# k' one slot sooner, token-MLP stages re-slotted, relu of k on ScalarE, tables by iota and ScalarE

## The chip, the cores and the metric

One core of a Trainium2 chip. The metric is device time in microseconds (us) of one execution; the median of a few executions is the kernel's time. A profiled execution gives the span (first to last instruction) and the times of the single instructions.

## What is computed

Two parts, for 8 batches of 576 tokens, 8 heads of 64. First linear attention with position weights:

```python
r = np.maximum(x, 0.0)                       # x is q or k
phi = np.concatenate([r * c, r * s], -1)     # c, s = cos, sin of (pi/2) * pos / S
kv  = einsum('bhsf,bhsd->bhfd', k_p, v);  z = k_p.sum(2)
x   = einsum('bhsf,bhfd->bhsd', q_p, kv) / (einsum('bhsf,bhf->bhs', q_p, z) + 1e-6)
```

Then, with x as batch x 576 x 512, a mixing over tokens and an output product:

```python
W_tok = scale * einsum('bsd,btd->bst', x @ w_q, x @ w_k)
out   = np.maximum(einsum('bst,btd->bsd', W_tok, x), 0.0) @ w_out
```

All inputs and the output are float32; the kernel computes in bf16 with float32 sums.

## The kernel before, in words

**Units of work.** A *slot* g is one pair of heads of one batch: 32 slots, four to a batch (Bc = g // 4 is the batch, r = g % 4 the place in it). Loads and the elementwise preparation go by halves H = g // 2, that is two slots at a time (16 halves).

**Preparation of a half** (lines 173 to 211). `relu_k` makes rk = relu(k) in bf16, `mul_k` multiplies rk by the table `cossin` on VectorE and gives k' (tile kp, bf16, 128x2304), `cast_v` gives v in bf16 in one of three v buffers, and `dup_q` writes relu(q) twice side by side (tile qd). In the loop before, relu_k, cast_v and dup_q of half H+2 all run on GpSimd (POOL), issued in slot 2H, and mul_k of half H+1 runs on VectorE (DVE) in slot 2H+1, after that slot's other VectorE work. rk, kp and qd have two buffers each, the raw inputs four.

**A slot** (lines 215 to 258). `qk_pe(g)` issues 18 small matmuls k'^T v (needs kp and v) and 18 transposes of qd into the one buffer qk_ps. VectorE then copies k'v out (kv_sb) and multiplies the transposed q by the table cst (qpt). `num(g-1)` issues 12 matmuls of the slot before, and VectorE takes the reciprocal (rec) and the product x_sb.

**The token MLP of a batch** (lines 260 to 355) goes in stages, each a group of matmuls into the PSUM tag m2, which has two buffers in turn, and one copy out of it on ScalarE (ACT): xT (transposes of x, one stage for each half of a batch), wk (x w_k, tile wkj), wq (tile wqT), kx (wkj^T x), mx (four stages: two row halves i by two column halves nh; the relu goes with the copy, tile mix_sb), and wout (row tiles of 128 output rows, four matmuls each, copied to o_sb and stored by two DMAs per row tile from SyncE, SP). A pair of batches has 9 row tiles, 4 in the even batch's share and 5 in the odd one's.

**The order** is the program's own: the loop of lines 378 to 420 sets which stage is issued in which slot, and every engine and the SP queue work strictly in that order. Before, in the slots of batch Bc: r=0 and r=1 have the four mx stages of batch Bc-2, one ahead and one behind qk_pe; xT (second half of the batch before) is in r=1, wk and wq in r=2, kx in r=3 with xT of this batch's first half; wout pieces of batch Bc-3 stand in r=0, 1 and 2. After the loop (lines 422 to 438) a tail finishes the rest: mx of batch 6, the wout pieces of batches 5, 6 and 7, and all MLP stages of batch 7. SP's queue holds in this order the loads (load(H+3) in each even slot) and the stores of the wout pieces.

**The start** (lines 84 to 155): loads, 16 warm-up matmuls, and the tables: POOL counts by iota, VectorE makes them into angles and spreads cosine and sine over the table, ScalarE takes the sine.

Of the kernel before, what the change touches and what calls it, by code (L numbers as in the profile page):

```python
# [24 lines left out]
def kernel(  # L25
# [10 lines left out]
    nc = tc.nc  # L36
# [58 lines left out]
    warm_up(16)  # L95

    wq_f = consts.tile([P, NDM, DH], FP32)
    wk_f = consts.tile([P, NDM, DH], FP32)
    wo_f = consts.tile([P, NDM, DM], FP32)

    ident = consts.tile([P, P], BF16)
    make_identity(nc, ident)

    r_i = consts.tile([P, C9], I32)
    nc.gpsimd.iota(r_i, pattern=[[1, C9]], base=0, channel_multiplier=C9)
    t_i = consts.tile([P, C9, D], I32)
    nc.gpsimd.iota(t_i, pattern=[[1, C9], [C9, D]], base=0, channel_multiplier=0)
    r_f = consts.tile([P, C9], FP32)
    nc.vector.tensor_copy(r_f, r_i)
    g5_f = consts.tile([P, C9], FP32)  # L110
    nc.vector.tensor_scalar(g5_f, r_f, float(S) - 0.5, float(S),
                            op0=ALU.is_ge, op1=ALU.mult)
    s_f = consts.tile([P, C9], FP32)
    nc.vector.tensor_sub(s_f, r_f, g5_f)
    coef = math.pi / 2.0 / S
    u_f = consts.tile([P, C9], FP32)
    nc.vector.tensor_scalar(u_f, s_f, -coef, math.pi / 2.0, op0=ALU.mult, op1=ALU.add)
    cos_t = consts.tile([P, C9, 1], FP32)
    sin_t = consts.tile([P, C9, 1], FP32)
    nc.scalar.activation(cos_t, u_f, AF.Sin, bias=0.0, scale=1.0)  # L120
    nc.scalar.activation(sin_t, s_f, AF.Sin, bias=0.0, scale=coef)
    cossin = consts.tile([P, C9, 2, D], BF16)
    nc.vector.tensor_copy(cossin[:, :, 0, :], cos_t.to_broadcast([P, C9, D]))
    nc.vector.tensor_copy(cossin[:, :, 1, :], sin_t.to_broadcast([P, C9, D]))

    t_f = consts.tile([P, C9, D], FP32)
    nc.vector.tensor_copy(t_f, t_i)
    nc.vector.tensor_scalar(t_f[0:64], t_f[0:64], -1.0, float(S),
                            op0=ALU.mult, op1=ALU.add)
    cst = consts.tile([P, C9, D], BF16)  # L130
    nc.scalar.activation(cst, t_f, AF.Sin, bias=0.0, scale=coef)
# [40 lines left out]

    def relu_k(H, lo, hi, eng):
        if lo == 0:
            rks[H] = prep.tile([P, 2, C9, D], BF16, name="rk")
        o = rks[H][:, lo:hi].rearrange("p r c d -> p r (c d)")
        if eng is nc.scalar:
            nc.scalar.activation(o, raw["k", H][:, lo:hi, :], AF.Relu)  # L178
        else:
            eng.tensor_scalar(o, raw["k", H][:, lo:hi, :], FMAX, 0.0,  # L180
                              op0=ALU.min, op1=ALU.max)
# [10 lines left out]
    def cast_v(H, lo, hi, eng):  # L192
        src = raw["v", H][:, lo:hi, :].rearrange("p r (c d) -> p r c d", c=C9)
        dst = v_bufs[H % 3][:, lo:hi, :, 0:D]
        if eng is nc.scalar:
            nc.scalar.copy(dst, src)
        else:
            eng.tensor_scalar(dst, src, 1.0, 1.0, op0=ALU.mult, op1=ALU.mult)  # L198

    def dup_q(H, lo, hi, eng):  # L200
        if lo == 0:
            qd[H] = prep.tile([P, 2, C9, 2, D], BF16, name="qd")
        n = hi - lo
        dst = qd[H][:, lo:hi].rearrange("p r c w d -> p (r c) w d")
        src = raw["q", H][:, lo:hi, :].rearrange(
            "p r (c d) -> p (r c) d", c=C9).unsqueeze(2).to_broadcast(
                [P, n * C9, 2, D])
        if eng is nc.scalar:
            nc.scalar.activation(dst, src, AF.Relu)
        else:  # L210
            eng.tensor_scalar(dst, src, FMAX, 0.0, op0=ALU.min, op1=ALU.max)  # L211
# [100 lines left out]
        kxs[b] = kx  # L312

    def mx(b, st, eng):
        i, nh = divmod(st, 2)
        hs = S // 2
        if b % 2 == 0 and st == 0:
            mixs[b // 2] = mixpool.tile([P, NDM, 2 * S], BF16, name="mix_sb")
        mix_sb = mixs[b // 2]
        mx_ps = m2_tile(FP32, "mx_ps")  # L320
        for r in range(2):
            dmc = 2 * r + i
            nc.tensor.matmul(  # L323
                mx_ps[:, r, 0:hs],
                kxs[b][64 * r:64 * r + 64, dmc * P:(dmc + 1) * P],
                wqTs[b][64 * r:64 * r + 64, nh, :], start=True, stop=True)
        c0 = (b % 2) * S + nh * hs
        dst = mix_sb.rearrange("p (r i) n -> p r i n", r=2)[:, :, i, c0:c0 + hs]
        if eng is nc.scalar:
            nc.scalar.activation(dst, mx_ps[:, :, 0:hs], AF.Relu, scale=scale_moe)  # L330
        else:
            eng.tensor_scalar(dst, mx_ps[:, :, 0:hs], scale_moe, 0.0,  # L332
                              op0=ALU.mult, op1=ALU.max)

    def wout(bp, rt0, n, engs):
        o_ps = m2_tile(FP32, "o_ps")
        o_sb = outpool.tile([P, 2, DM], FP32, name="o_sb")
        for r in range(n):
            rt = rt0 + r
            for dmc in range(NDM):  # L340
                nc.tensor.matmul(  # L341
                    o_ps[:, r, :], mixs[bp][:, dmc, rt * P:(rt + 1) * P],
                    wo_sb[:, dmc, :], start=(dmc == 0), stop=(dmc == NDM - 1))
        if len(engs) == 1:
            copy(engs[0], o_sb[:, 0:n, :], o_ps[:, 0:n, :])
        else:
            for r in range(n):
                copy(engs[r], o_sb[:, r, :], o_ps[:, r, :])
        for r in range(n):
            for hi in range(2):  # L350
                bloc, j0 = divmod(P * (rt0 + r) + 64 * hi, S)
                dst = dataclasses.replace(
                    out, offset=out.offset + (2 * bp + bloc) * S * DM + (j0 // 64) * DM,
                    ap=[[C9 * DM, 64], [1, DM]])
                nc.sync.dma_start(dst, o_sb[hi * 64:hi * 64 + 64, r, :])
# [84 lines left out]

# [28 lines left out]
```

## Time and profile before

| what | value |
|---|---|
| median of 3 executions | 162.76 us (161.47 to 163.2) |
| profiled execution, its own time | 162.92 us |
| its span | 161.1 us (1.8 us lie around it) |
| busy in the span: PE, DVE, ACT, POOL | 119.4, 100.9, 72.3, 75.0 us |
| mean granted TensorE clock | 0.906 |
| start of qk_pe in slots 4, 6, 8 | 23.82, 32.63, 42.10 us |
| start of qk_pe in slots 12, 16, 20, 24, 28 | 56.60, 70.86, 87.11, 102.78, 118.95 us |
| start of num(31), the first work of the tail | 131.75 us |

A row of the time line reads: start, duration, engine, line and operation, output<-inputs, and in square brackets how long the engine had been idle before it and what ended that. PE is TensorE, SPq is SyncE's queue of DMA issues. "x18" at a row's end means 18 instructions merged.

### The profile page before, as it was taken

Reading aid. Unit: us, or ns where it says so; the run is one execution under the profiler, and the core shown is the slowest. Engines: PE = TensorE matmul, PEld = TensorE weight load, DVE = VectorE, ACT = ScalarE, POOL = GpSimd, SP = SyncE. Lnnn points to the kernel's source line nnn. Section 1 sums busy time; section 2 is a strip of 40 time slices with the busy share of each in tenths; the row PEclk is TensorE's granted clock in tenths of the full one; section 3 lists DMA queues with packets and bytes.
Section 4 is the critical chain, followed back from the end, with each engine's and each line's share of the span. In section 5 each row is a group of like instructions: output and inputs, shape, how many; then the busy total and the mean of one; then the engine's idle time right before and its main releaser. Section 6 shows DMA issues by size and latency. Waiting matters only on the chain.

```text
span 161.1 us, 5016 instructions
## 1 busy us (share of the span) xinstructions
PE 119.4 (74%) x2184; PEld 78.6 (49%) x2184; DVE 100.9 (63%) x163; ACT 72.3 (45%) x96; POOL 75.0 (47%) x68
## 2 busy tenths in 40 slices
PE   6633655599649798979994969797979986996920
PEld 2222654486437555755663537454645663452400
DVE  6668684954794858776757678767576766024210
ACT  3422420211841547475645553764476653634320
POOL 7188269998665556632995366456520000000000
PEclk9995586556995999999999999999999999999996
DMA  5999999999994005499969989995521540278785
GB/s 174 379 379 377 404 412 411 408 410 406 409 402 172 0 4 131 94 285 406 375 140 344 401 322 216 375 410 178 118 51 36 124 109 0 57 164 204 164 194 132
DMA packets 20469, 39.38 MB, mean 244 GB/s; under 512 B 3040, under 2 KB 3040, under 8 KB 20448
## 3 DMA queue, kind: packets, MB, share of 16 engines
q1 hardware_dynamic: 20448, 39.07, 72.6%
q8 instruction: 17, 0.28, 0.7%
q14 instruction: 4, 0.03, 0.1%
HBM read 29.62 MB, written 9.44 MB: 242 GB/s over the span
## 4 chain that ended last, share of the span: by engine, by line
PE 42%; DVE 29%; ACT 7%; DMA 6%; SPq 5%; POOL 3%; issue 3%; ACTq 0%; POOLq 0%
DVE kp L187 14%; PE o_ps L341 14%; DVE x_sb L256 7%; PE qk_ps L223 6%; PE wq_ps L296 6%; DMA kf<-in_k_dram 6%; ACT o_sb L274 5%; PE num_ps L250 5%; PE qk_ps L230 4%; DVE qpt_buf L237 4%; PE wk_ps L282 4%; SPq L81 3%; PE mx_ps L323 2%; POOL qd L211 2%; DVE kv_sb L235 2%
## 5 line engine op out<-in xcount | busy, mean ns | idle before, releaser
L211 POOL TENSOR_SCALAR qd<-qf 128x2304 bf16<-128x2304 f32 (+1 forms) x16 | 33.7, 2109 | 10.2 <-issue 8.6
L223 PE MATMUL qk_ps<-v_buf,kp 64*128 64x65 bf16 x576 | 15.9, 201 | 25.1 <-DVE kp L187 21.3
L341 PE MATMUL o_ps<-wo_sb,mix_sb 128*128 128x512 bf16 x144 | 33.7, 379 | 0.1
L187 DVE TENSOR_TENSOR kp<-rk,cossin 128x2304 bf16<-128x2304 bf16 (+1 forms) x17 | 29.4, 1727 | 2.2 <-ACT rk L178 2.2
L235 DVE CAST kv_sb<-qk_ps 128x130 bf16<-128x130 f32 x32 | 9.4, 293 | 33.1 <-PE qk_ps L230 33.1
L223 PEld LDWEIGHTS <-kp 64*128 64x128 bf16 x576 | 12.3, 100 | 33.2 <-DVE kp L187 26.4
L198 POOL TENSOR_SCALAR v_buf<-vf 128x1152 bf16<-128x1152 f32 (+1 forms) x17 | 20.8, 1222 | 15.8 <-DMA vf<-in_v_dram 15.0
L256 DVE TENSOR_TENSOR x_sb<-num_ps,rec 128x640 bf16<-128x640 f32 x32 | 26.4, 825 | 1.1
L274 ACT COPY o_sb<-o_ps 128x1024 f32<-128x1024 f32 (+1 forms) x20 | 17.6, 885 | 20.7 <-PE o_ps L341 20.7
L180 POOL TENSOR_SCALAR rk<-kf 128x1152 bf16<-128x1152 f32 x15 | 17.7, 1180 | 16.0 <-DVE kp L187 10.3
L237 DVE TENSOR_TENSOR qpt_buf<-qk_ps,cst 128x1152 bf16<-128x1152 bf16 x32 | 23.9, 748 | 0.0
L274 ACT COPY xT_buf<-xT_ps 128x1152 bf16<-128x1152 bf16 x15 | 16.8, 1119 | 13.0 <-PE xT_ps L266 13.0
L330 ACT ACTIVATE mix_sb<-mx_ps 128x576 bf16<-128x576 f32 x28 | 17.7, 654 | 6.7 <-PE mx_ps L323 6.6
L341 PEld LDWEIGHTS <-mix_sb 128*128 128x128 bf16 x144 | 13.4, 98 | 14.1 <-issue 0.5
L250 PE MATMUL num_ps<-kv_sb,qpt_buf 128*128 128x65 bf16 x320 | 17.9, 204 | 0.1
L230 PE MATMUL qk_ps<-ident,qd 64*128 64x64 bf16 x576 | 15.3, 200 | 1.5 <-POOL qd L211 1.5
L250 PEld LDWEIGHTS <-qpt_buf 128*128 128x128 bf16 x320 | 13.7, 103 | 3.2 <-DVE x_sb L256 0.4
L323 PE MATMUL mx_ps<-wqT,kx 64*128 64x288 bf16 x64 | 9.1, 288 | 5.3 <-ACT o_sb L274 2.7
L230 PEld LDWEIGHTS <-qd 64*128 64x128 bf16 x576 | 12.1, 101 | 1.6 <-POOL qd L211 1.6
L266 PE MATMUL xT_ps<-ident,x_sb 128*128 128x128 bf16 x160 | 12.3, 228 | 0.7 <-DVE mix_sb L332 0.7
L266 PEld LDWEIGHTS <-x_sb 128*128 128x128 bf16 x160 | 10.5, 103 | 2.6 <-issue 0.9
L253 PE MATMUL num_ps<-eps_t,ones_t 128*128 128x5 bf16 x64 | 11.2, 176 | 0.0
(52 smaller groups left out, 105.1 us busy)
## 6 DMA issues: line engine op xcount, KB each, us to landing
out_dram<-o_sb SPq DMA_DIRECT2D x72, 128.0 KB, 2.4
kf<-in_k_dram SPq DMA_DIRECT2D x15, 576.0 KB, 9.3
qf<-in_q_dram SPq DMA_DIRECT2D x15, 576.0 KB, 9.6
vf<-in_v_dram SPq DMA_DIRECT2D x15, 576.0 KB, 9.8
wo_f<-in_moe_w_out_dram SPq DMA_DIRECT2D x1, 1024.0 KB, 9.9
kf<-in_k_dram SPq DMA_DIRECT2D x2, 288.0 KB, 3.5
qf<-in_q_dram SPq DMA_DIRECT2D x2, 288.0 KB, 4.0
vf<-in_v_dram SPq DMA_DIRECT2D x2, 288.0 KB, 4.2
```

Source lines behind the costliest of these rows:

```text
L180: eng.tensor_scalar(o, raw["k", H][:, lo:hi, :], FMAX, 0.0, op0=ALU.min, op1=ALU.max)
L187: nc.vector.tensor_mul(kp[H][:, lo:hi], rks[H][:, lo:hi].unsqueeze(3).to_broadcast([P, n, C9, 2, D]), cossin.unsqueeze(1).to_broadcast([P, ...
L198: eng.tensor_scalar(dst, src, 1.0, 1.0, op0=ALU.mult, op1=ALU.mult)
L211: eng.tensor_scalar(dst, src, FMAX, 0.0, op0=ALU.min, op1=ALU.max)
L223: nc.tensor.matmul(kvp[:, hh, :], kp[H][p0:p0 + 64, i, c, :, :], v_bufs[H % 3][p0:p0 + 64, i, c, 0:D + 1], start=(c == 0), stop=(c == C9 - 1))
L230: nc.tensor.transpose(qt[:, hh, c * D:(c + 1) * D], qd[H][p0:p0 + 64, i, c, :, :], ident[p0:p0 + 64, p0:p0 + 64])
L237: nc.vector.tensor_mul(qpt_bufs[g % 3][:, :, 1:SLOTS, :], qt.rearrange("f h (c d) -> f h c d", c=C9), cst.unsqueeze(1).to_broadcast([P, 2, ...
L250: nc.tensor.matmul(nv[:, hh, u, :], qpt_bufs[g % 3][:, hh, 2 * u:2 * u + 2, :], kvs[g][:, hh, :], start=(u == 0), stop=False)
L256: nc.vector.tensor_tensor(xs[b][:, :, 2 * pr:2 * pr + 2, :].rearrange("p u h d -> p h u d"), nv[:, :, :, 0:D], rec.to_broadcast([P, 2, SC, ...
L266: nc.tensor.transpose(xT_ps[:, i, u * P:(u + 1) * P], xs[b][:, u, 2 * hp:2 * hp + 2, :], ident)
L274: nc.scalar.copy(dst, src)
L341: nc.tensor.matmul(o_ps[:, r, :], mixs[bp][:, dmc, rt * P:(rt + 1) * P], wo_sb[:, dmc, :], start=(dmc == 0), stop=(dmc == NDM - 1))
```

## The change

Five edits:

1. `mul_k(H+1)` moves from slot 2H+1 to slot 2H, that is one slot ahead.
2. In the loop relu_k goes to ScalarE; POOL keeps dup_q, now ahead of cast_v. In the first half of the data dup_q goes to POOL and cast_v to VectorE; relu_k of half 1 goes to ScalarE.
3. The MLP stages move: mx of a batch stands in r=3 of the next batch (two stages, column half 0) and in r=0 after it (two, column half 1), behind qk_pe; wk in r=1 behind a wout piece, kx and wq in r=2. The numbering of mx's stages changes so that the first two fill column half 0.
4. The wout pieces of batch Bc-2 (not Bc-3) stand in r=0 (2 row tiles), r=1 (1) and r=3 (1 or 2). The tail therefore loses the five row tiles of batch 5 and two mx stages, and its order changes.
5. The tables are made from iotas by two sine activations on ScalarE with the counts as int32 inputs; eight VectorE instructions fall away. 14 warm-up matmuls, not 16.

```diff
+    for hh in range(2):
+        ph = slice(64 * hh, 64 * hh + 64)
+        nc.gpsimd.iota(ki[ph, :, 0], pattern=[[-1, C9]], base=S, channel_multiplier=-C9)
+        nc.gpsimd.iota(ki[ph, :, 1], pattern=[[1, C9]], base=0, channel_multiplier=C9)
+    nc.gpsimd.iota(qi[0:64], pattern=[[-1, C9], [-C9, D]], base=S, channel_multiplier=0)
+    nc.gpsimd.iota(qi[64:128], pattern=[[1, C9], [C9, D]], base=0, channel_multiplier=0)
...
+    nc.scalar.activation(cossin, ki.unsqueeze(3).to_broadcast([P, C9, 2, D]),
+                         AF.Sin, bias=0.0, scale=coef)
+    nc.scalar.activation(cst, qi, AF.Sin, bias=0.0, scale=coef)
...
     def mx(b, st, eng):
-        i, nh = divmod(st, 2)
+        nh, i = divmod(st // 2 + 2 * (st % 2), 2)
...
     for lo in range(2):
         relu_k(0, lo, lo + 1, A)
-        cast_v(0, lo, lo + 1, G)
-        dup_q(0, lo, lo + 1, A if lo == 0 else G)
+        dup_q(0, lo, lo + 1, G)
+        cast_v(0, lo, lo + 1, V)
         mul_k(0, lo, lo + 1)
     load(2)
-    relu_k(1, 0, 2, G)
+    relu_k(1, 0, 2, A)
+    dup_q(1, 0, 2, G)
     cast_v(1, 0, 2, G)
-    dup_q(1, 0, 2, G)
...
-            return [(bp, 0, 2), (bp, 2, 2)]
-        return [(bp, 4, 2), (bp, 6, 2), (bp, 8, 1)]
+            return [(bp, 0, 2), (bp, 2, 1), (bp, 3, 1)]
+        return [(bp, 4, 2), (bp, 6, 1), (bp, 7, 2)]
...
-        if r == 0 and Bc >= 2:
-            mx(Bc - 2, 0, A)
-        if r == 1 and Bc >= 2:
-            mx(Bc - 2, 2, A)
         qk_pe(g)
-        if r == 0 and Bc >= 2:
-            mx(Bc - 2, 1, A)
-        if r == 1 and Bc >= 2:
-            mx(Bc - 2, 3, A)
+        if r == 3 and Bm >= 0:
+            mx(Bm, 0, A)
+            mx(Bm, 2, A)
+        if r == 0 and Bm >= 1:
+            mx(Bm - 1, 1, A)
+            mx(Bm - 1, 3, A)
         if g >= 1:
             num(g - 1)
-        if g % 2 == 1 and H + 1 < NB:
+        if g % 2 == 0 and H + 1 < NB:
             mul_k(H + 1, 0, 2)
...
-            relu_k(H + 2, 0, 2, G)
+            relu_k(H + 2, 0, 2, A)
+            dup_q(H + 2, 0, 2, G)
             cast_v(H + 2, 0, 2, G)
-            dup_q(H + 2, 0, 2, G)
...
+        if r == 0:
+            wout_piece(Bm - 1, 0)
         if r == 1:
...
+            if Bm >= 0:
+                xT(2 * Bm + 1, A)
+            wout_piece(Bm - 1, 1)
+            if Bm >= 0:
+                wk_stage(Bm, A)
+        if r == 2 and Bm >= 0:
+            kx_stage(Bm, A)
+            wq_stage(Bm, A)
         if r == 3:
...
+            wout_piece(Bm - 1, 2)
             xT(2 * Bc, A)
+    L = B - 1
     num(NG - 1)
+    mx(L - 1, 1, A)
+    mx(L - 1, 3, V)
+    wout_piece(L - 1, 0)
+    xT(2 * L + 1, V)
+    wout_piece(L - 1, 1)
+    wk_stage(L, V)
+    wout_piece(L - 1, 2)
+    wq_stage(L, A)
+    kx_stage(L, V)
+    for st in (0, 2, 1, 3):
+        mx(L, st, A if st < 2 else V)
+    for w in ((L // 2, 4, 2), (L // 2, 6, 2), (L // 2, 8, 1)):
         wout(*w, (A, V))
```

(Bm is Bc - 1; `wout_piece(b, n)` issues the n-th piece of batch b on ScalarE, if b is not negative.)

How it moves the instructions, at three places. First VectorE in slots 4 and 5 (halves: kp here is that of half 3, needed by slot 6). Before:

```order
L235 CAST kv_sb<-qk_ps 128x130
L237 TENSOR_TENSOR qpt_buf_158<-qk_ps,cst 128x2x576
L255 RECIPROCAL rec<-num_ps 128x10
L256 TENSOR_TENSOR x_sb<-num_ps,rec 128x2x5x64
L235 CAST kv_sb<-qk_ps 128x130
L237 TENSOR_TENSOR qpt_buf_160<-qk_ps,cst 128x2x576
L255 RECIPROCAL rec<-num_ps 128x10
L256 TENSOR_TENSOR x_sb<-num_ps,rec 128x2x5x64
L187 TENSOR_TENSOR kp<-rk,cossin 128x2304
L235 CAST kv_sb<-qk_ps 128x130
```

and with the change, for the same two slots:

```order
L221 CAST kv_sb<-qk_ps 128x130
L223 TENSOR_TENSOR qpt_buf_144<-qk_ps,cst 128x2x576
L241 RECIPROCAL rec<-num_ps 128x10
L242 TENSOR_TENSOR x_sb<-num_ps,rec 128x2x5x64
L173 TENSOR_TENSOR kp<-rk,cossin 128x2304
L221 CAST kv_sb<-qk_ps 128x130
L223 TENSOR_TENSOR qpt_buf_146<-qk_ps,cst 128x2x576
L241 RECIPROCAL rec<-num_ps 128x10
L242 TENSOR_TENSOR x_sb<-num_ps,rec 128x2x5x64
L221 CAST kv_sb<-qk_ps 128x130
```

The k' product stood behind all work of slot 5 and directly ahead of the kv_sb copy of slot 6; now it stands at the end of slot 4, with the four instructions of slot 5 between it and slot 6.

Second, ScalarE in the four slots that hold the wout pieces of batch 1 (o_sb): slots 16 to 19 before, from the mx copies of r=0 on:

```order
L330 ACTIVATE mix_sb<-mx_ps 128x2x288 x2
L274 COPY o_sb<-o_ps 128x1024
L330 ACTIVATE mix_sb<-mx_ps 128x2x288 x2
L274 COPY xT_buf_164<-xT_ps 128x2x576
L274 COPY o_sb<-o_ps 128x1024
L274 CAST wkj<-wk_ps 128x640
L274 CAST wqT<-wq_ps 128x576
L274 COPY o_sb<-o_ps 128x512
L274 CAST kx<-kx_ps 128x512
L274 COPY xT_buf_162<-xT_ps 128x2x576
```

and slots 12 to 15 now:

```order
L316 ACTIVATE mix_sb<-mx_ps 128x2x288 x2
L164 ACTIVATE rk<-kf 128x1152
L260 COPY o_sb<-o_ps 128x1024
L260 COPY xT_buf_148<-xT_ps 128x2x576
L260 COPY o_sb<-o_ps 128x512
L260 CAST wkj<-wk_ps 128x640
L164 ACTIVATE rk<-kf 128x1152
L260 CAST kx<-kx_ps 128x512
L260 CAST wqT<-wq_ps 128x576
L316 ACTIVATE mix_sb<-mx_ps 128x2x288 x2
L260 COPY o_sb<-o_ps 128x1024
L260 COPY xT_buf_150<-xT_ps 128x2x576
```

The two relu of k (rk) are new on ScalarE, one in r=0 between the mx copies and the wout copy, one in r=2 ahead of kx; and the output of batch 1 is copied four slots sooner.

Third, ScalarE at the end of the program, from the mx copies of batch 6 on. Before:

```order
L330 ACTIVATE mix_sb<-mx_ps 128x2x288 x2
L274 COPY o_sb<-o_ps 128x1024 x2
L274 COPY o_sb<-o_ps 128x512
L274 CAST wqT<-wq_ps 128x576
L274 COPY o_sb<-o_ps 128x1024 x2
L330 ACTIVATE mix_sb<-mx_ps 128x2x288 x2
L274 COPY o_sb<-o_ps 128x512 x3
```

and now:

```order
L316 ACTIVATE mix_sb<-mx_ps 128x2x288
L260 COPY o_sb<-o_ps 128x1024
L260 COPY o_sb<-o_ps 128x512 x2
L260 CAST wqT<-wq_ps 128x576
L316 ACTIVATE mix_sb<-mx_ps 128x2x288 x2
L260 COPY o_sb<-o_ps 128x512 x3
```

Three wout copies of batch 5 and one of the ScalarE mx copies of batch 6 are gone from the tail; the three last copies, of batch 7's output, are the same.

More of the change, by code (lines that the diff above doesn't have):

```diff
@@ L99 @@
     wo_f = consts.tile([P, NDM, DM], FP32)
+    coef = math.pi / 2.0 / S
+    ki = consts.tile([P, C9, 2], I32)
+    qi = consts.tile([P, C9, D], I32)
+    for hh in range(2):
[4 more added lines that the diff above has]
+    nc.gpsimd.iota(qi[64:128], pattern=[[1, C9], [C9, D]], base=0, channel_multiplier=0)
@@ L101 @@
+    cossin = consts.tile([P, C9, 2, D], BF16)
+    cst = consts.tile([P, C9, D], BF16)
+    nc.scalar.activation(cossin, ki.unsqueeze(3).to_broadcast([P, C9, 2, D]),
+                         AF.Sin, bias=0.0, scale=coef)
+    nc.scalar.activation(cst, qi, AF.Sin, bias=0.0, scale=coef)
     ident = consts.tile([P, P], BF16)
     make_identity(nc, ident)
-    r_i = consts.tile([P, C9], I32)
-    nc.gpsimd.iota(r_i, pattern=[[1, C9]], base=0, channel_multiplier=C9)
-    t_i = consts.tile([P, C9, D], I32)
@@ L107 @@
[L107 to L131, printed above, removed]
     ones_t = consts.tile([P, P], BF16)
@@ L373, in wouts, with wout_piece @@
         if b % 2 == 0:
-            return [(bp, 0, 2), (bp, 2, 2)]
-        return [(bp, 4, 2), (bp, 6, 2), (bp, 8, 1)]
+            return [(bp, 0, 2), (bp, 2, 1), (bp, 3, 1)]
+        return [(bp, 4, 2), (bp, 6, 1), (bp, 7, 2)]
+    def wout_piece(b, n):
+        if b >= 0:
+            wout(*wouts(b)[n], (A,))
     NG = 2 * NB
```

32 lines of the change are left out of this document (2 added, 30 removed).

## The prediction

> **What bounds the kernel now.** I read the page's chain first, then the waits, then the windows of the loop and of the tail, then single slots in the time line.
>
> ```profile
> span 161.1 us, 5016 instructions
> PE 42%; DVE 29%; ACT 7%; DMA 6%; SPq 5%; POOL 3%; issue 3%; ACTq 0%; POOLq 0%
> ```
>
> ```profile
> PE qk_ps L223 <- DVE kp L187: 21.3, 14, 3.7
> POOL v_buf L198 <- DMA vf<-in_v_dram: 15.0, 7, 3.3
> ```
>
> The chain that ends last alternates between TensorE and VectorE. TensorE's great wait is for one product: 14 times, 21.3 us in all, the first matmuls of a slot wait for kp (k'). POOL waits 15.0 us for v, but it stands little in the chain (3%).
>
> ```profile
> 60.56 2.11 POOL L211 TENSOR_SCALAR qd<-qf 128x2304 bf16<-128x2304 f32 x1 [1.56 <-issue]
> 62.51 1.36 DVE L187 TENSOR_TENSOR kp<-rk,cossin 128x2304 bf16<-128x2304 bf16 x1
> 63.94 0.46 PE L223 MATMUL qk_ps<-v_buf,kp 64*128 64x65 bf16 x18 [0.15 <-DVE kp L187]
> ...
> 92.48 2.11 POOL L211 TENSOR_SCALAR qd<-qf 128x2304 bf16<-128x2304 f32 x1
> 93.07 2.73 DVE L187 TENSOR_TENSOR kp<-rk,cossin 128x2304 bf16<-128x2304 bf16 x1
> 95.86 0.46 PE L223 MATMUL qk_ps<-v_buf,kp 64*128 64x65 bf16 x18 [1.52 <-DVE kp L187]
> ```
>
> Two slots of one kind (14 and 22 are both r=2): kp stands last on VectorE, directly ahead of the slot that needs it. Alone it takes 1.36 us. Where POOL is within its qd it takes 2.73: POOL ends at 94.59, and 94.59 + 1.3 is 95.8, so kp in effect starts when POOL ends. TensorE waits 0.15 us in one case, 1.52 in the other.
>
> ```profile
> 42.10:131.75 89.65, 75.41 (x1604) 50.97 (x1605) 64.91 (x107) 48.73 (x65) 45.17 (x30) 0.98 0.67 221
> 131.75:161.10 29.35, 18.45 (x129) 8.96 (x127) 7.64 (x11) 10.75 (x15) 0.00 (x0) 0.95 0.55 127
> ```
>
> The columns are stretch, length, then busy time of PE, PEld, DVE, ACT, POOL, then clock, DMA share and GB/s. From slot 8 to the end of the slots (batches 2 to 7) TensorE is busy 75.41 of 89.65 us: 14.2 us idle, 2.4 a batch. In the tail it works 18.45 of 29.35. So there are three parts, which I sum separately: the start up to slot 8 (42.1 us), six batches (89.65) and the tail (29.35). Together they are the span.
>
> **k' one slot sooner.** kp now ends a whole slot ahead of its use. Its work does not shrink (1.36 us alone, twice a batch); it hides behind the next slot's matmuls. VectorE has room: 64.91 busy of 89.65 us. It also meets POOL less: POOL loses relu, and its qd can begin only when the transposes of the slot after have freed the buffer, about when kp ends. If the cover went, each kp would cost up to 1.52 us again. What is late next is TensorE itself, so the six batches are priced by its own work.
>
> **Five row tiles of output move from the tail into the loop.** In the six batches 22 row tiles (88 matmuls) become 27.
>
> ```profile
> 42.10:131.75 89.65, 20.94 (x88) 0.98 0.67 221
> ```
>
> ```profile
> 149.57 4.49 PE L341 MATMUL o_ps<-wo_sb,mix_sb 128*128 128x512 bf16 x20
> ```
>
> 88 matmuls in 20.94 us or 20 in 4.49 us both give 0.9 to 0.95 us a row tile of four. I take 0.9: five tiles are 4.5 us. TensorE's work in the batches is then 75.4 + 4.5 = 79.9 us.
>
> **The new waits there.** All MLP stages share two PSUM buffers in turn, and ScalarE empties every one of them in the loop, now with relu k in between.
>
> ```profile
> L274 ACT COPY xT_buf<-xT_ps 128x1152 bf16<-128x1152 bf16 x15 | 16.8, 1119 | 13.0 <-PE xT_ps L266 13.0
> L274 ACT COPY o_sb<-o_ps 128x1024 f32<-128x1024 f32 x14 | 14.2, 1013 | 17.5 <-PE o_ps L341 17.5
> L330 ACT ACTIVATE mix_sb<-mx_ps 128x576 bf16<-128x576 f32 x28 | 17.7, 654 | 6.7 <-PE mx_ps L323 6.6
> L209 ACT ACTIVATE qd<-qf 128x1152 bf16<-128x1152 f32 x1 | 1.1, 1147 | 0.0
> ```
>
> ```profile
> 133.01 0.30 PE L323 MATMUL mx_ps<-wqT,kx 64*128 64x288 bf16 x2 [0.52 <-ACT xT_buf L274]
> ```
>
> relu k has no such row on ScalarE at full size; the nearest, a relu of 1152 output elements, took 1.147 us. Twice a batch that is 2.3 us, 13.8 in six: ScalarE goes from 48.73 to about 62 plus the moved copies, of some 86. It is not the bound, but its order matters. In r=3 the wout copy (1.01) and the xT copy (1.12) stand ahead of the second mx of r=0, and TensorE reaches that mx about 1.4 us after xT's matmuls end: with one row tile it waits some 0.3 us, with two 0.7. The row at 133.01 shows this wait in the tail of before, 0.52 us. In r=1 wk waits for the same kind of copy behind one row tile: 1.12 - 0.9, some 0.3 with the handoff. I take 1.0 us a batch, 6.0 in all; the bounds are 0.2 a batch (as in slot 14 above, 0.15) and today's 2.4. Six batches: 79.9 + 6.0 = 85.9 us, for 89.65.
>
> **The start.**
>
> ```profile
> 21.39 1.15 POOL L198 TENSOR_SCALAR v_buf<-vf 128x1152 bf16<-128x1152 f32 x1 [1.50 <-DMA vf<-in_v_dram]
> 22.62 3.11 POOL L211 TENSOR_SCALAR qd<-qf 128x2304 bf16<-128x2304 f32 x1
> 25.78 0.66 PE L230 MATMUL qk_ps<-ident,qd 64*128 64x64 bf16 x18 [1.50 <-POOL qd L211]
> 32.63 0.68 PE L223 MATMUL qk_ps<-v_buf,kp 64*128 64x65 bf16 x18 [2.19 <-DVE kp L187]
> ```
>
> ```profile
> 26.00:42.10 16.10, 12.54 (x229) 9.84 (x224) 11.05 (x18) 4.28 (x6) 13.81 (x9) 0.60 1.04 408
> ```
>
> The tables and the two warm-up matmuls end before the data and are worth nothing here: half 2's v lands at 21.39 whatever is done before, and the DMA engines are saturated (share 1.04). Then things move. qd now goes ahead of the v copy, so only a copy of 1.15 us follows the landing and the 1.50 us wait of slot 4 goes; the 2.19 us wait of slot 6 goes with the earlier kp. Against that, relu k on ScalarE waits for each k as it lands, and holds the xT copies behind it. At most 1.5 plus the 3.56 us idle of the last row (16.10 - 12.54) can be won, at least 0.5. I take half: 2.6, so slot 8 starts at 39.5 us.
>
> **The tail.** It loses the five row tiles (4.5 us) and two mx stages, whose waits are 0.52 us in the row above and about as much again: 1.0 in all. But kx's copy is no longer covered by a row-tile pair ahead of the mx stages, which costs about 0.3 more than today's waits. 29.35 - 4.5 - 1.0 + 0.3 = 24.1 us; bounds 23 and 26. The last five row tiles and the final copy and store are unchanged.
>
> **Sum.** 39.5 + 85.9 + 24.1 = 149.5 us of span. Around the profiled span lie 1.8 us (162.92 - 161.1); that execution is 0.1% above the median. 151.3 us, 7% faster.
>
> **Rivals.**
>
> *The idle time stays.* kp's wait goes and the wait for the two PSUM buffers takes its place in full: idle 14.2 us as today, so 39.5 + 79.9 + 14.2 + 24.1 = 157.7, with what lies around 159.5 us. For it: ScalarE now has relu in r=0 ahead of the wout copy. Against it: the copies' durations above add up to fewer waits.
>
> *A warmer clock at the start.*
>
> ```profile
> 34.00:36.00 2.00, 2.00 (x34) 1.82 (x32) 1.74 (x4) 0.40 (x1) 2.00 (x2) 0.50 1.04 411
> 38.00:40.00 2.00, 2.00 (x39) 1.39 (x34) 1.35 (x4) 0.17 (x1) 1.37 (x2) 0.80 1.04 408
> 40.00:42.00 2.00, 1.09 (x14) 0.64 (x11) 2.00 (x2) 1.73 (x3) 0.83 (x1) 1.00 1.05 415
> ```
>
> The clock was at half until TensorE had worked about 5 us without a gap (from 33.1), then full at 40. If the waits at 25.78 and 32.63 go, that run of work begins near 24 and the clock is full near 30, so some 8 us of TensorE work ahead of slot 8 go at double pace: 4 us less, 147.3 us. Against it: the gaps may simply be elsewhere, since data still come every 4 us.
>
> The Trainium skill (TensorE: Matmul & The Clock Gate, Part 1) says that the clock doubles after about 3.4 us of sustained work and falls back after an idle window of that length. By that rule this rival would be the likelier the fewer gaps are left; the trace agrees in kind, with 5 rather than 3.4 us.
>
> *Slower: k arrives late at ScalarE.* relu k stands in ScalarE's strict order ahead of kx (r=2) and of the wout copy (r=0). If k is late, every copy out of PSUM behind it waits, and TensorE with it.
>
> ```profile
> 84.46 1.30 SPq L355 DMA_DIRECT2D out_dram<-o_sb  x2
> 97.94 0.54 SPq L81 DMA_DIRECT2D kf<-in_k_dram  x1
> 102.81 1.15 POOL L180 TENSOR_SCALAR rk<-kf 128x1152 bf16<-128x1152 f32 x1 [1.29 <-DVE kp L187]
> ```
>
> ```profile
> kf<-in_k_dram SPq DMA_DIRECT2D x15, 576.0 KB, 9.3
> ```
>
> A load is issued two slots (some 7 us) ahead, less the four stores ahead of it on SP (0.65 us each) and the copy they wait for: some 4.5 us of lead. With the median of 9.3 us from issue to landing each k would be 4.8 us late; for the seven late halves, with two thirds of it on the path, 22 us less about 7 that the longer slots give back: 151.3 + 15 = 166 us. It decides from a landing of 4.5 us on. Against it: in the loop the k issued at 97.94 was there by 102.81 (its relu waited for kp, not for the DMA), and most of the 9.3 come from the saturated start.
>
> **How the numbers follow.** My sum 0.55; the idle time stays 0.18; warm clock 0.17; late k 0.10. The range takes all but the last: from 144.5 (warm clock, and waits near their lower bound) to 159.5. A measurement of this kernel can tell about 1% from no change. Faster by over 1% is all but the last case and a little of the second: 0.87; within 1% 0.04; slower 0.09.
>
> **What would show it.** Right: the waits for kp are gone from TensorE's list (under 3 us, from 21.3); qk_pe of slot 8 near 39.5, the tail begins near 125.4, and batches last 13.5 to 15 us; TensorE's waits name the ScalarE copies of xT and o_sb. Wrong: ScalarE's rk rows idle before them on the DMA of k (late k); batches still near 15.6 us (idle stays); clock at 1.00 from 30 us on (warm). If TensorE still waits for kp, the change does not do what it says.

## The result, and the profile after

| | before | with the change |
|---|---|---|
| median | 162.42 us (4 executions, 161.47 to 163.2) | 150.82 us (4, 150.18 to 152.03) |
| ratio | | 0.9297, interval 0.9211 to 0.9383 |
| profiled execution, span, mean clock | 162.92, 161.1 us, 0.906 | 151.38, 149.6 us, 0.934 |

The forecast was 151.3 us, in a range of 144.5 to 159.5. Here and in the experiments the medians take all executions of a kernel, while the ratios and their intervals leave out slow ones, those over 1.5% above its fastest. The three parts of the span, from the starts of slot 8's qk_pe (L209) and of num(31) (L236):

| part | before | forecast | after |
|---|---|---|---|
| start, up to slot 8 | 42.10 | 39.5 | 37.67 |
| batches 2 to 7 | 89.65 | 85.9 | 87.22 |
| tail | 29.35 | 24.1 | 24.7 |
| span | 161.1 | 149.5 | 149.6 |

The sum is right to 0.1 us, the parts are not: 1.8 us too much in the start, 1.3 too little in the batches, 0.6 too little in the tail. They cancel, so the closeness of the sum is luck; four executions of the change alone lie 1.9 us apart.

First the list of TensorE's waits over the whole program (what waits, for what; us in all, times, longest):

```profile
PE qk_ps L209 <- POOL v_buf L184: 7.2, 2, 4.1
PE mx_ps L309 <- ACT xT_buf L260: 3.9, 7, 0.7
PE wk_ps L268 <- ACT xT_buf L260: 3.2, 7, 1.1
...
PE qk_ps L209 <- DVE kp L173: 0.7, 1, 0.7
```

The wait for kp is down to 0.7 us, from 21.3. The longest is now for v, and it lies ahead of slot 8. The same list for the six batches alone names what the forecast named, the ScalarE copies:

```profile
PE mx_ps L309 <- ACT xT_buf L260: 3.2, 6, 0.7
PE wk_ps L268 <- ACT xT_buf L260: 2.1, 6, 0.3
PE o_ps L327 <- ACT mix_sb L316: 1.0, 6, 0.2
PE mx_ps L309 <- ACT wqT L260: 1.0, 1, 1.0
```

Then the windows (length, busy time of PE, PEld, DVE, ACT, POOL, then clock, DMA share, GB/s): the six batches, the tail, batch 2 alone and batch 5 alone.

```profile
37.67:124.89 87.22, 78.36 (x1604) 53.02 (x1627) 60.91 (x108) 61.91 (x82) 34.22 (x22) 1.00 0.83 265
124.89:149.60 24.71, 13.56 (x105) 7.10 (x103) 6.97 (x10) 8.16 (x12) 0.00 (x0) 0.94 0.53 117
37.67:51.51 13.84, 12.61 (x268) 8.61 (x271) 10.60 (x19) 10.51 (x14) 7.30 (x6) 1.00 0.92 287
80.45:96.05 15.60, 13.46 (x271) 9.06 (x275) 10.32 (x18) 10.45 (x15) 7.38 (x5) 1.00 0.95 327
```

TensorE's idle time in the batches fell from 14.2 to 8.9 us. VectorE lost 4.0 us of work (64.91 to 60.91). The groups by line say where: kp alone has 4.8 us less. Its rows, in the batches of before, then of after (count, busy time, mean ns):

```profile
L187 DVE TENSOR_TENSOR kp<-rk,cossin 128x2304 bf16<-128x2304 bf16 x11 | 19.6, 1784 | 0.0
```

```profile
L173 DVE TENSOR_TENSOR kp<-rk,cossin 128x2304 bf16<-128x2304 bf16 x11 | 14.8, 1349 | 0.0
```

The same product takes 1349 ns in the mean, not 1784: it no longer runs beside qd. The time line of after, in batch 4, shows them one behind the other, since qd waits for the transposes of the slot that follows kp:

```profile
69.66 1.35 DVE L173 TENSOR_TENSOR kp<-rk,cossin 128x2304 bf16<-128x2304 bf16 x1
71.18 2.11 POOL L197 TENSOR_SCALAR qd<-qf 128x2304 bf16<-128x2304 f32 x1 [4.97 <-PE qk_ps L216]
```

The start. Time line around slots 4 to 8:

```profile
20.42 1.36 DVE L173 TENSOR_TENSOR kp<-rk,cossin 128x2304 bf16<-128x2304 bf16 x1 [1.20 <-ACT rk L164]
20.82 2.93 POOL L197 TENSOR_SCALAR qd<-qf 128x2304 bf16<-128x2304 f32 x1 [4.79 <-DMA qf<-in_q_dram]
23.82 1.15 POOL L184 TENSOR_SCALAR v_buf<-vf 128x1152 bf16<-128x1152 f32 x1
25.03 0.68 PE L209 MATMUL qk_ps<-v_buf,kp 64*128 64x65 bf16 x18 [4.09 <-POOL v_buf L184]
25.49 0.70 PE L216 MATMUL qk_ps<-ident,qd 64*128 64x64 bf16 x18
27.24 0.68 PE L209 MATMUL qk_ps<-v_buf,kp 64*128 64x65 bf16 x18 [0.35 <-DVE qpt_buf L223]
32.02 0.46 PE L209 MATMUL qk_ps<-v_buf,kp 64*128 64x65 bf16 x18
35.19 0.46 PE L209 MATMUL qk_ps<-v_buf,kp 64*128 64x65 bf16 x18
37.67 0.46 PE L209 MATMUL qk_ps<-v_buf,kp 64*128 64x65 bf16 x18
```

Slot 4's transposes of qd start only 0.3 us sooner than before (25.49, behind the 18 products k'^T v from 25.03 on; before 25.78). qd stands beside kp and takes 2.93 us, and the v copy, ready or not, stands behind qd. So the 1.50 us wait that the forecast removed, and the 1.73 us for kp that stood ahead of slot 4's products in before, became one wait of 4.09 us ahead of the whole qk_pe. The won time comes later: from slot 6 to slot 8 before took 9.47 us (32.63 to 42.10), now 5.65 (32.02 to 37.67). One reason shows in the durations themselves: slot 6's 18 matmuls take 0.46 us here, and 0.68 in before. The windows say the same by their clock column:

```profile
30.00:32.00 2.00, 0.90 (x22) 0.70 (x20) 1.69 (x4) 1.12 (x1) 1.96 (x1) 0.82 1.05 388
32.00:34.00 2.00, 1.95 (x55) 1.46 (x54) 1.18 (x4) 1.67 (x2) 1.15 (x1) 1.00 1.06 392
```

Full clock from about 31 us on, where before had it from about 39. That is the warm-clock rival, in part: slots 6 and 7 ran at the full clock.

And the late k, in batch 5 (15.60 us, where batches 3 and 7, which also hold five row tiles, took 14.70 and 14.60). SyncE's queue, then the engines:

```profile
82.14 0.58 SPq L81 DMA_DIRECT2D kf<-in_k_dram  x1
```

```profile
90.41 1.16 ACT L164 ACTIVATE rk<-kf 128x1152 bf16<-128x1152 f32 x1 [1.85 <-DMA kf<-in_k_dram]
90.94 0.46 PE L209 MATMUL qk_ps<-v_buf,kp 64*128 64x65 bf16 x18
91.48 0.57 ACT L260 CAST kx<-kx_ps 128x512 bf16<-128x512 f32 x1
91.94 0.64 ACT L260 CAST wqT<-wq_ps 128x576 bf16<-128x576 f32 x1
92.64 0.42 PE L309 MATMUL mx_ps<-wqT,kx 64*128 64x288 bf16 x4 [0.98 <-ACT wqT L260]
```

k lands some 8.3 us after its issue; ScalarE stands 1.85 us in front of it, kx and wqT behind it are late, and TensorE's mx waits 0.98 us. The slower rival's mechanism exists, once in six batches, for about 0.9 us. All ten relus of the batches, by line:

```profile
L164 ACT ACTIVATE rk<-kf 128x1152 bf16<-128x1152 f32 x10 | 11.7, 1172 | 2.2 <-DMA kf<-in_k_dram 2.2
```

ScalarE was idle for k for 2.2 us ahead of all of them together, 1.85 of it in the row above.

### The profile page after: what moved, and what is told of

The parts are those of the page before. It is cut to its first block, busy times and chain, and to the rows that moved or that the text cites. A ratio compares the mean times of both kernels' runs of the same rounds, so it can differ in the third digit from the quotient of the medians.

```text
span 149.6 us, 4978 instructions
## 1 busy us (share of the span) xinstructions
PE 115.7 (77%) x2155; PEld 77.5 (52%) x2182; DVE 90.6 (61%) x156; ACT 88.1 (59%) x114; POOL 56.8 (38%) x56
## 5 line engine op out<-in xcount | busy, mean ns | idle before, releaser
L197 POOL TENSOR_SCALAR qd<-qf 128x2304 bf16<-128x2304 f32 (+1 forms) x17 | 35.6, 2092 | 52.1 <-PE qk_ps L216 30.6
L164 ACT ACTIVATE rk<-kf 128x1152 bf16<-128x1152 f32 (+1 forms) x17 | 18.9, 1111 | 18.4 <-DMA kf<-in_k_dram 9.2
L260 ACT COPY o_sb<-o_ps 128x512 f32<-128x512 f32 (+1 forms) x24 | 18.4, 765 | 17.9 <-PE o_ps L327 8.3
L209 PE MATMUL qk_ps<-v_buf,kp 64*128 64x65 bf16 x576 | 15.8, 199 | 11.0 <-POOL v_buf L184 7.2
L173 DVE TENSOR_TENSOR kp<-rk,cossin 128x2304 bf16<-128x2304 bf16 (+1 forms) x17 | 22.2, 1305 | 1.6 <-ACT rk L164 1.6
L209 PEld LDWEIGHTS <-kp 64*128 64x128 bf16 x576 | 11.9, 99 | 17.2 <-issue 8.7
L184 POOL TENSOR_SCALAR v_buf<-vf 128x1152 bf16<-128x1152 f32 x15 | 17.3, 1151 | 1.2
L236 PE MATMUL num_ps<-kv_sb,qpt_buf 128*128 128x65 bf16 x320 | 17.4, 202 | 0.0
L236 PEld LDWEIGHTS <-qpt_buf 128*128 128x128 bf16 x320 | 13.4, 102 | 3.6 <-issue 1.7
L216 PE MATMUL qk_ps<-ident,qd 64*128 64x64 bf16 x576 | 14.8, 197 | 0.0
L309 PE MATMUL mx_ps<-wqT,kx 64*128 64x288 bf16 x64 | 8.0, 285 | 7.0 <-ACT xT_buf L260 3.9
```

The lines of the kernel that those rows point to most:

```text
L173: nc.vector.tensor_mul(kp[H][:, lo:hi], rks[H][:, lo:hi].unsqueeze(3).to_broadcast([P, n, C9, 2, D]), cossin.unsqueeze(1).to_broadcast([P, ...
L209: nc.tensor.matmul(kvp[:, hh, :], kp[H][p0:p0 + 64, i, c, :, :], v_bufs[H % 3][p0:p0 + 64, i, c, 0:D + 1], start=(c == 0), stop=(c == C9 - 1))
L216: nc.tensor.transpose(qt[:, hh, c * D:(c + 1) * D], qd[H][p0:p0 + 64, i, c, :, :], ident[p0:p0 + 64, p0:p0 + 64])
L236: nc.tensor.matmul(nv[:, hh, u, :], qpt_bufs[g % 3][:, hh, 2 * u:2 * u + 2, :], kvs[g][:, hh, :], start=(u == 0), stop=False)
```

## The experiments

All times are medians; the ratio is to the kernel before on the same chip. The runs come from several chips, on which before itself took 162.14 to 163.46 us, so small differences between two experiments are safer read from the ratios. The main theory: k' one slot sooner takes away the kp wait and is the larger part; the shorter lag takes row tiles out of the tail and pays for them in the loop; relu on ScalarE and the tables are worth nothing.

**k' late again.** The change with mul_k back in the odd slot.

```diff
-        if g % 2 == 0 and H + 1 < NB:
+        if g % 2 == 1 and H + 1 < NB:
             mul_k(H + 1, 0, 2)
```

> The changed kernel with one edit: mul_k goes back to the odd slot. Theory (TensorE sets the pace of the batches once k' is out of its way): kp stands again directly ahead of the slot that needs it, TensorE waits 0.5 to 1 us for it in 12 to 14 halves, 157 us (154 to 161), and the waits list names kp again with 6 us or more. Rival (the shorter tail and the new places of the MLP stages brought the gain): 152 us or less, kp waits under 2 us.

160.99 us, ratio 0.9884 (0.9804 to 0.9964). Its waits and its six batches:

```profile
PE qk_ps L209 <- DVE kp L173: 12.6, 14, 3.5
```

```profile
42.50:134.16 91.66, 78.80 (x1603) 52.82 (x1628) 62.19 (x107) 61.28 (x81) 43.42 (x21) 1.00 0.75 233
```

The wait for kp is back, 14 times. Against the change: start +4.8 (42.50), batches +4.4, tail the same (24.64). So the one moved instruction is worth 10.2 us of the 11.6 in this order of work (9.5 us of 11.4 by the ratios), more than I expected. All other edits together, without it, bring 1.2% (0.4 to 2.0). The start's gain hangs on it in this trace: without it slot 8 starts at 42.50, as in before. The windows of its start show how:

```profile
30.00:32.00 2.00, 0.85 (x20) 0.73 (x18) 1.97 (x4) 1.12 (x1) 1.69 (x1) 0.99 1.03 386
32.00:34.00 2.00, 0.74 (x27) 0.62 (x25) 1.63 (x1) 1.03 (x2) 1.92 (x2) 0.86 1.07 395
34.00:36.00 2.00, 1.98 (x45) 1.56 (x41) 1.08 (x3) 0.82 (x1) 0.64 (x1) 0.50 1.04 388
```

The clock rises here too, by 30 us. But then wk waits 1.15 us for an xT copy and slot 6 waits 1.26 us for kp, TensorE is busy 0.74 of 2 us, and the clock falls back to half. In the change's profile wk waits as well (1.10 us), slot 6 does not, and the clock stays up (1.95 busy from 32 to 34, clock 1.00).

**k' sooner alone.** The kernel before with the opposite edit.

```diff
-        if g % 2 == 1 and H + 1 < NB:
+        if g % 2 == 0 and H + 1 < NB:
             mul_k(H + 1, 0, 2)
```

> The kernel before with one edit: mul_k one slot sooner, all else as before. Theory: the 12.0 us of waits for kp in batches 2 to 7 and some 3 us ahead of them vanish, part of it turns into waits for copies out of PSUM; 153.5 us (152 to 157). Rival (the gain is in the tail and the stages): 160 us or more.

156.2 us, before 163.46. Its four executions lie between 152.68 and 157.68, too far apart for an interval; the profiled one took 156.85. It has a part of its own that costs it some 3 us (an estimate: the gap below, and half of the 3.3 us at half clock behind it):

```profile
100.34 0.17 PE L253 MATMUL num_ps<-eps_t,ones_t 128*128 128x5 bf16 x1 [1.58 <-issue]
```

```profile
98.00:100.00 2.00, 0.73 (x13) 0.51 (x13) 1.25 (x3) 1.07 (x2) 0.00 (x0) 1.00 1.01 392
...
102.00:104.00 2.00, 2.00 (x6) 0.60 (x4) 0.00 (x0) 0.24 (x1) 2.00 (x2) 0.50 0.96 352
```

TensorE stands still for 1.58 us ahead of a tiny matmul whose inputs are constants, with nothing that the profile names, and the clock falls to half behind it. What sets the other three executions apart is not shown. With that said, k' alone is worth 7.3 us by the medians and 9.0 by the best executions (152.68 against 161.64), most of the 11.6.

**The old lag.** The change, with each wout piece one batch later; the tail takes the five row tiles back.

```diff
-            wout_piece(Bm - 1, 0)
+            wout_piece(Bm - 2, 0)
...
-            wout_piece(Bm - 1, 1)
+            wout_piece(Bm - 2, 1)
...
-            wout_piece(Bm - 1, 2)
+            wout_piece(Bm - 2, 2)
...
     mx(L - 1, 3, V)
+    for n in range(3):
+        wout_piece(L - 2, n)
```

> The changed kernel with the output row tiles one batch later again: five row tiles go back into the tail. Theory (the batches are bound by TensorE, so the row tiles cost there what they cost in the tail): only the tail's waits come back, 152 us (151 to 153); the batches are 4.5 us shorter and the tail 5 to 6 longer. Rival (the loop had room for them): the tail is 5 us longer and the batches are no shorter, 155.5 us.

156.91 us, 0.9636 (0.9573 to 0.9698). A miss: the rival was nearer. The lag is worth 6.1 us with the early k' (5.5 by the ratios). With the old lag the kernel is no faster than k' alone (156.2), so nothing shows that the other edits add to these two. The parts say why the lag pays: start 37.44, batches 85.95 (only 1.3 less than the change, with five row tiles fewer), tail 31.61 (6.9 more). Each of the two profiles has a stall of its own in batch 5, the late k there and a gap of 1.41 us here. Set against the repeat of the change below, which has no late k (86.38), and without the gap, the five row tiles cost 1.8 us in the batches. Batch 2, which here has no row tile at all, and the tail:

```profile
37.44:50.49 13.05, 9.51 (x254) 7.25 (x253) 11.88 (x19) 8.56 (x11) 7.50 (x5) 1.00 1.05 390
...
123.39:155.00 31.61, 19.81 (x124) 9.39 (x123) 6.98 (x10) 10.17 (x15) 0.00 (x0) 0.92 0.57 125
```

In batch 2 TensorE is busy 9.51 of 13.05 us, in the change 12.61 of 13.84: four row tiles more cost 0.8 us there, not 3.6. In the old lag's batch 2 it is VectorE that is busy nearly throughout (11.88 of 13.05). Its time line, and a row of the tail:

```profile
40.27 2.11 POOL L197 TENSOR_SCALAR qd<-qf 128x2304 bf16<-128x2304 f32 x1 [1.09 <-PE qk_ps L216]
40.50 3.08 DVE L173 TENSOR_TENSOR kp<-rk,cossin 128x2304 bf16<-128x2304 bf16 x1
...
44.51 0.46 PE L209 MATMUL qk_ps<-v_buf,kp 64*128 64x65 bf16 x18 [0.87 <-DVE qpt_buf L223]
...
142.35 6.16 PE L327 MATMUL o_ps<-wo_sb,mix_sb 128*128 128x512 bf16 x20 [0.51 <-ACT mix_sb L316]
```

Here kp meets qd again (3.08 us) and the next qk_pe waits behind it. So there was room in that batch, and the row tiles filled it. The last row belongs to the tail: its last 20 output matmuls took 6.16 us where the change's took 4.48, at a lower clock (0.76 from 142 to 149 us, 1.00 in the change from 138 to 142.5), so 1.7 of the tail's 6.9 us are clock and not row tiles.

**relu of k on GpSimd.** The change with relu_k of the loop on POOL.

```diff
-            relu_k(H + 2, 0, 2, A)
+            relu_k(H + 2, 0, 2, G)
```

> The changed kernel with relu k of the loop on GpSimd again. Theory: kp has room of a slot, so meeting GpSimd costs TensorE nothing, and ScalarE has fewer copies to delay: 150 to 152 us. Rival (freeing VectorE from GpSimd was the gain): kp near 1.8 us in the mean and TensorE late with it, 155 us or more.

152.09 us, 0.9316 (0.9234 to 0.9397); the change itself has 0.9297. Batches of 13.84 to 14.86 us, 87.06 in all, the same as the change's 87.22. As expected: the move is worth nothing that shows, in either direction. kp takes 1348 ns in the mean here too, so it was not relu's leaving POOL that made it shorter. Slot 6 meets only the half clock in this trace (0.50 from 31 to 34 us), though it waits for nothing, and slot 8 starts at 38.63:

```profile
32.05 0.68 PE L209 MATMUL qk_ps<-v_buf,kp 64*128 64x65 bf16 x18
```

**xT copies on VectorE.** To take the two waits for ScalarE's xT copy away.

```diff
-            xT(2 * Bc, A)
+            xT(2 * Bc, V)
```

(and the same for the other xT of the loop)

> The changed kernel with the xT copies of the loop on VectorE (0.76 us each there, 1.12 on ScalarE). Theory (what is left of TensorE's idle time in the batches is the emptying of two PSUM buffers by ScalarE, 5.3 of 8.9 us behind xT copies): these waits go, 147 us (145.5 to 148.5). Rival (VectorE is strict in order too and has kv_sb behind the copy): 151 to 154 us, with waits of TensorE for qpt or kv_sb in their place.

154.74 us, 0.9509 (0.9429 to 0.9589). A miss, and on the other side. The waits of the profile:

```profile
PE wk_ps L268 <- ACT o_sb L260: 4.3, 6, 0.7
```

The waits of mx for xT are down to 0.2 us, but wk now waits 4.3 us, and by the program's order that is for the copy on VectorE, which stands behind x_sb:

```profile
32.50 0.70 PE L268 MATMUL wk_ps<-wk_sb,xT_buf 128*128 128x64 bf16 x18 [2.17 <-DVE xT_buf L262]
...
88.65 0.82 DVE L242 TENSOR_TENSOR x_sb<-num_ps,rec 128x640 bf16<-128x640 f32 x1
89.39 0.75 DVE L262 COPY xT_buf<-xT_ps 128x1152 bf16<-128x1152 bf16 x1
...
90.09 0.80 PE L268 MATMUL wk_ps<-wk_sb,xT_buf 128*128 128x64 bf16 x20 [0.72 <-ACT o_sb L260]
```

(The list names o_sb, which ends at 90.04; the xT copy, which wk reads, ends at 90.14, with wk right at it. The rows can't separate the two.) The batches last the same as in the change, 87.15 us in all. What is lost is the start: slot 8 at 40.42, 2.75 us later. wk of batch 0 waited 2.17 us for such a copy (first row), 1.1 more than in the change, and behind it the clock was at 0.50 from 34 to 37 us, where the change has 1.00.

**Filler matmuls.** Ten matmuls ahead of slot 2 and ten ahead of slot 4, to keep the clock full, each ten into one turn of the two buffers of m2; their output is not used.

```diff
+        if g in (2, 4):
+            fill(10)
         qk_pe(g)
```

> The changed kernel with ten idle matmuls of 512 columns ahead of slot 2 and ten ahead of slot 4, into a buffer that nobody reads, so that TensorE has no long gaps while it waits for v. Theory (the start was won by the clock, full from about 31 us on and not from 39): the clock is full earlier, slots 5 to 7 are shorter, 149 to 150.5 us. Rival (the start follows the landing of the data): 150.5 to 152 us.

150.89 us, 0.9264 (0.9171 to 0.9357): no gain over the change. The clock did rise, 0.979 over the span:

```profile
6.95:24.80 17.85, 9.20 (x210) 6.06 (x211) 10.54 (x18) 5.88 (x8) 9.36 (x5) 1.00 1.06 381
24.80:37.02 12.22, 10.25 (x249) 8.26 (x250) 10.65 (x18) 8.35 (x10) 8.13 (x5) 0.86 1.05 391
```

Full clock up to slot 4, yet slot 4 starts at 24.81 and slot 8 at 37.02, 0.2 and 0.65 us sooner than in the change. The fillers did not hold the clock beyond that: it was at 0.50 from 27 to 29 us, and slot 5's products took 0.68 us as in the change. The DMA share is 1.05 throughout, so up to slot 4 the start waits for data and not for the clock.

**Loads one half sooner.** Five raw buffers and load(H+4), against the late k.

```diff
-        if g % 2 == 0 and H + 3 < NB:
-            load(H + 3)
+        if g == 0:
+            load(3)
+        if g % 2 == 0 and H + 4 < NB:
+            load(H + 4)
```

> The changed kernel with every load one half sooner in SP's queue (load(H+4) in place of load(H+3)) and five raw buffers in place of four. Theory (late k holds ScalarE's copies in the one batch of 15.6 us): ScalarE's waits for k in the batches go from 2.2 us to nothing and that batch comes to 14.7 us: 149.3 us (148.5 to 150.5). Rival (the wait for k is slack): 150.8 us.

150.54 us, 0.9243 (0.9155 to 0.9332). Batches 13.84, 14.71, 14.24, 14.71 and 14.24 us: the late k is gone from its trace, 86.35 us for all six. No gain clear of the spread, and theory and rival stay undecided: in the repeat of the change below ScalarE did not wait for k either, while in the traces of k' late again, the old lag, xT copies on VectorE, fillers and old tables it waited 1.0 to 2.8 us. (The profile is of its slowest execution, 152.79, and slot 8 starts at 39.94 there, with slot 6 at half clock.)

**The old tables,** with 16 warm-up matmuls.

```diff
-    warm_up(14)
+    warm_up(16)
```

(and the tables' code of before in place of the new)

> The changed kernel with the tables made as before (and 16 warm-up matmuls). Theory: they end before the data that they meet, so nothing changes: 150.3 to 151.3 us. Rival (the first half waits for the tables): 1 to 2 us longer, 152 to 153 us.

150.64 us, 0.9253 (0.9143 to 0.9362). Worth nothing that shows, as expected.

**num between the mx stages, and xT ahead of num.** The PSUM tag m2 has two buffers; in r=0 the two mx stages follow each other at once and wait for ScalarE's xT copy. Here num stands between them, and in r=1 xT goes ahead of num, so that its copy has the time of num and a row tile before wk.

```diff
         if r == 0 and Bm >= 1:
             mx(Bm - 1, 1, A)
-            mx(Bm - 1, 3, A)
+        if r == 1 and Bm >= 0:
+            xT(2 * Bm + 1, A)
         if g >= 1:
             num(g - 1)
+        if r == 0 and Bm >= 1:
+            mx(Bm - 1, 3, A)
...
-            if Bm >= 0:
-                xT(2 * Bm + 1, A)
             wout_piece(Bm - 1, 1)
```

> The changed kernel with two places of TensorE's order exchanged: in r=0 num stands between the two mx stages, in r=1 xT stands ahead of num, so that TensorE has num's 0.44 us to do while ScalarE's xT copy frees the PSUM buffer. Theory (the waits for xT copies, 3.2 us ahead of mx and 2.1 ahead of wk in the batches, are on the path): most of them go, 147 us (146 to 148.5), batches of 13.2 and 14.1 us. Rival (as with the copies on VectorE, the wait turns up at the next buffer): 150 us or more, batches as in the changed kernel.

149.63 us, 0.9219 (0.9157 to 0.928). On that chip the change itself, run again, took 150.55:

> The changed kernel as it is, on the chip of the other three, as their measure: 150.8 us (150 to 152).

0.9333 (0.9278 to 0.9387). The six batches of the two, first this experiment, then the change again:

```profile
37.72:121.62 83.90, 80.63 (x1628) 54.16 (x1627) 60.90 (x108) 62.55 (x82) 34.24 (x22) 1.00 0.85 276
```

```profile
37.62:124.00 86.38, 79.69 (x1629) 52.97 (x1627) 60.83 (x108) 61.93 (x82) 34.22 (x22) 1.00 0.83 269
```

2.5 us less: 3.3 us of idle time are left of 6.7, and the records show 0.9 us more of busy time. Only 0.9 us of it show in the median, less than expected: its six executions spread from 147.97 to 150.72, and the intervals of the two just touch. In the profile the tail gave 1.2 us back, at a clock of 0.90 against 0.93.

**Both together,** the last order with the loads one half sooner, and then with the fillers too.

> The same with each load one half sooner and five raw buffers. Theory: the one batch that waits for k loses its 1.4 us, and nothing else: 1 us below the kernel without this edit. Rival: the earlier loads take DMA time from the data that the start waits for, and what the batch wins is lost ahead of slot 8: the same time.

> The same with both edits and the idle matmuls ahead of slots 2 and 4. Theory (the start varies by 3 us with the moment at which the clock comes back, and the filling fixes that moment): slot 8 starts at 37 to 37.5 us, 1 to 2 us below the kernel without the filling. Rival (data bound start): the same time.

148.46 us, 0.916 (0.9103 to 0.9216), and 148.53, 0.9157 (0.9108 to 0.9206). The first beats the change too: its interval lies wholly under that of the change on the same chip (0.9278 to 0.9387), by about 2.1 us. Slot 8 starts at 37.59 and the batches take 84.17 us. What the earlier loads add to the new order is not shown: the median is 1.2 us lower, but the intervals overlap and the batches are no shorter (83.90 without them). The fillers add nothing again, a miss: slot 8 starts at 37.12, as expected, but without them it started at 37.59.

## Why the prediction was right, and where it was not

*The kp wait goes: right.* 21.3 us became 0.7, and putting mul_k back brings 12.6 us of it and 10.2 us of time back. In the batches the wait vanished outright (12.0 us in before, none after). Of the 9.2 us of it ahead of slot 8 most changed only its name: TensorE waits 7.2 us for v there. What I named as cover held: VectorE had room, and kp meets POOL's qd less (1784 to 1349 ns). Of the two reasons that I gave for that, the qd that begins only after the transposes is the one that counts; with relu back on POOL kp is as short.

*TensorE's own work then sets the batches: right in kind.* I had 79.9 us of work; the repeat of the change, whose records miss fewer matmuls than the first profile's (1629, not 1604), shows 79.69. The waits were put at 6.0 us in all; that repeat has 6.69 idle, and the first profile 8.86, of which 0.8 to 0.9 are the late k and 1.3 matmuls whose records are missing. The names were right: 0.5 a batch for mx (I had 0.3 to 0.7), 0.35 for wk (I had 0.3).

*Five row tiles cost 4.5 us in the loop: right for TensorE, wrong as time.* Compared with the old lag they lengthen the batches by 1.3 us, or 1.8 without the two stalls. The term took a batch with free room (batch 2, where four row tiles cost 0.8) as if it were full; the sum held all the same, because it was made from TensorE's total work and not from before's batches plus 4.5. It shows in what the shorter lag is worth: not a mere shift of work from tail to loop (my expectation for that experiment had little left), but 6.1 us.

*The start: the step failed.* "The 1.50 us wait of slot 4 goes" did not happen: I put qd ahead of v and priced only the v copy behind the landing, but qd itself came late and long (20.82, 2.93 us beside kp), and v had to stand behind it. The wait moved from the transposes to the products in front of them. The gain of 4.4 us, where I had 2.6, came from the step that I had put at 2.19, the earlier kp of slot 6, and from the clock. Without the earlier kp the start is 42.50. But the early kp does not by itself keep the clock: in the traces of relu on POOL, early loads and old tables slot 6 waits for no kp and still has the half clock, and slot 8 starts at 38.63, 39.94 and 38.70. In the first of them slot 6 starts at 32.05, as in the change (32.02), so about 1 us of the 1.8 by which the start beat my forecast hangs on the clock of that execution. With the fillers, which kept the clock full up to slot 4, slot 8 came 0.65 us sooner; slot 5 was at half clock all the same, so they do not say what a full clock there would give.

*The tail: 24.7 for 24.1.* Both bounds hold. kx's copy on the path was named and priced at 0.3; the row for it shows 0.86. I had taken 0.7 us of waits off in sum, but the waits of TensorE in the tail add up to 3.8 us before and after, and that is about the size of the miss:

```profile
135.94 0.42 PE L309 MATMUL mx_ps<-wqT,kx 64*128 64x288 bf16 x4 [0.86 <-DVE kx L262]
...
138.01 4.48 PE L327 MATMUL o_ps<-wo_sb,mix_sb 128*128 128x512 bf16 x19 [0.51 <-ACT mix_sb L316]
```

*The rivals.* "Idle stays" did not come; idle fell by 5.4 us. The warm clock came for slots 6 and 7, not from slot 4 on. (My reading of before's clock was short: TensorE worked from 32.63 without a gap and the clock came back near 38.8, after some 6 us and not 5.) The late k came once, with a landing of 8.3 us. It costs 0.9 us and not the 15 I gave it: I had put the lead at 4.5 us, and ScalarE stood ready for this k only 6.4 us after its issue; the median landing of k was 6.7 us and not 9.3; most relus in the loop wait for no load (2.2 us in all ten).

*Still open.* What the unnamed gaps ahead of single small matmuls are (1.58 us in k' sooner alone, 1.41 in the old lag). Whether the early k' is worth as much in before's order as in the new one: 7.3 to 9.0 against 9.5 to 10.2 us does not tell. And what decides in a given run whether slot 6 meets the full clock: with relu on POOL it did not (slot 8 at 38.63), in the change and its repeat it did (37.67 and 37.62).

## What to carry to other kernels

When TensorE waits for an instruction that stands last on an engine with room, move that one instruction a whole stage ahead and look at what else it was running beside: here one line was most of the gain, in the wait itself, in a shorter product and, in some executions, in an earlier full clock. Before pricing work that moves from a tail into a loop at its full duration, ask in which of the loop's stages the receiving engine is idle. And where two buffers go round between one engine and its copier, put other work of the first engine between two stages that share them; here that shortened the batches by 2.5 us, and the copies on VectorE, 0.75 us each for 1.1 on ScalarE, did not shorten them.

## What the runs showed that I had not expected

- The clock fell to 0.50 after a gap of 1.58 us with a thin stretch before it (TensorE busy 0.73 of 2 us) in k' sooner alone, and after a wait of 1.26 us (busy 0.74 of 2 us) in k' late again. The Trainium skill (TensorE: Matmul & The Clock Gate, Part 1) gives an idle window of about 3.4 us for the fall. In these two traces it fell with shorter gaps. In k' late again there were two of them in a row: TensorE was busy 0.7 of the 3.1 us ahead of slot 6.
- A product on VectorE took 3.08 us beside GpSimd's qd, 1.35 alone, and qd 2.93 beside the product against 2.11 alone: in these rows whichever began later paid. The Trainium skill (SBUF — State Buffer, Terms) describes a pair of ports that the two engines hold for a whole instruction; these rows agree to 0.15 us. So the order of two engines that never wait for each other by the program can cost as much as a wait.
- A full clock can be worth little: with the DMA share at 1.05, the fillers' full clock up to slot 4 started that slot 0.2 us sooner.
